# Output-weight sums on GpSimd, with later releases of their places and an earlier left sum

## The chip, the cores and the metric

The kernel runs on one core of one Trainium2 chip, in float32. The metric is the device time of one execution in microseconds (us). PE is TensorE, DVE is VectorE, ACT is ScalarE, POOL is GpSimd, SP is the engine whose queue issues the loads and stores spoken of here.

## The reference

Eight sequences of 448 rows go through an attention with 12 heads of 64, whose queries and keys are normalised, and then through a feed-forward network with a gate.

```python
def _attn_ref(q, k, v, g_q, g_k):                 # (8, 12, 448, 64)
    q_n, k_n = rmsnorm(q, g_q), rmsnorm(k, g_k)
    attn = softmax(q_n @ k_n.T / sqrt(64))
    return attn @ v

# bridge: (B,H,S,D) -> (B*S, H*D), 3584 x 768

def _moe_ref(x, w_gate, w_val, w_out, rms_g):     # 768 -> 1536 -> 768
    xn = x / rms(x) * rms_g
    g = xn @ w_gate
    return (silu(g) * (xn @ w_val)) @ w_out
```

## The kernel before

The function `safe_scores` writes the whole program in an order made by hand: each engine gets its instructions in the order in which the Python code emits them. `pe(fn)` emits one step of TensorE work and advances a counter `now["t"]`; `after(n, fn)` keeps a function back until n steps later. While the attention of one sequence is emitted, `fill` puts steps of the feed-forward network of the sequence before it between the attention's steps, so that TensorE always has work. The times below name these stages by what TensorE is doing for the network.

**Gate and value.** Sequence 0 uses the plain product. From sequence 1 on, four groups of columns are each computed by 15 block products in place of 18 (`PRODUCTS`, `three`, `product`, L1182). Nine of the 15 right operands are sums of weight blocks. They are made once, during sequence 1, by `derive` on DVE (L1087, L1090), stored to the DRAM scratch `kept` (L1095) and loaded from there by the later sequences. The left operands are sums of blocks of x, kept ready in the list `slow`.

**Output projection.** The stage of sequences 1 and 4 uses seven products in place of eight (`out_strassen`, L1447). Their right operands are the blocks B11, B21, B22 of the output weights and four sums T1 to T4. These sums, 4 for each of 6 columns, are made by `derive_o` (L1122) during sequence 1's gate stage and stored to `kept_o` by `keep` (L952). Their left operands are sums made from the list `first_sums` (16 of them in sequence 1, L1364, emitted from the end of the gate stage on), one after each step. Sequences 2, 3, 5, 6 and 7 apply the seven products once more inside each product (`out_quads`, L1518). Their right operands, the four-tile sums, are made by `derive_q` (L1150 to L1153) in 21 units of four subtractions, each followed by four stores to `kept_q` (L1157, L1160). The left operands S1 to S4 of that inner level are made by `left_q1` (L1392). For the tile i its steps come in the order a(i), d(i−1), b(i), c(i); d needs S4.

**Places and the load queue.** Weight blocks live in an arena of places. `ask` runs down a fixed list of loads (`uses`) and issues the next one on SP when `room(keep_free + 1)` says that enough places are free; it does so from `used`, one step or three after a place was given back by `give_back`. The list holds each sequence's gate loads (`wg`), then its output loads (`wo`, or `wq` for the two-level form). Loads of T sums wait until the sum's store has been emitted. The sources of the output sums (`wd`) and of the four-tile sums (`wx`) are loaded from another list, `side` (L1046); the loads of `uses` are L1066. Loads and stores share SP's queue, in order, and a store that waits for its data holds whatever stands behind it.

**The order inside `fill`.** After each step, `fill` makes at most one of the left sums, then `derive` if the attention's block began more than two steps ago, and, more than four steps after the block began, two `derive_o` if no `derive` was made, and one `derive_q`. `derive_q` returns at once while any output sum is still to be made.

Of the kernel before, what the change touches and what calls it, by code (L numbers as in the profile page):

```python
# [12 lines left out]
ALU = mybir.AluOpType  # L13
# [322 lines left out]
def safe_scores(  # L336
# [20 lines left out]
    nc = tc.nc  # L357
# [16 lines left out]
    st = {}  # L374


    now, due = {"t": 0}, []

    def after(n, fn):
        due.append((now["t"] + n, fn))  # L380
# [396 lines left out]
    slow, first_sums = [], []  # L777
# [109 lines left out]
    def data(key):  # L887
        return st[key][0][:, 0:GW if key[0] == "wg" else BW]
# [137 lines left out]
    asked = {"n": 0, "derived": 0}  # L1026
# [4 lines left out]
    derived = [(g, to) for g in GROUPS for _, _, to in PRODUCTS if to in RIGHT_G]  # L1031
# [6 lines left out]
    def ask():  # L1038

        if turn_of["n"] < TURNS:  # L1040
            return
        while side and (room(1, "side") or side[0][0] == "wd" and asked["derived"] > 32 and room(4, "wg")):
            key = side.pop(0)
            asked[key] = now["t"]
            st[key] = block("side" if room(1, "side") else "wg")
            nc.sync.dma_start(out=data(key), in_=home(key))  # L1046
        while asked["n"] < len(uses):
            key = uses[asked["n"]]
            kind, keep_free = "wg" if key[0] == "wg" else "w", 3
            if key[1] == 1 and key[0] == "wg":  # L1050
                kind, keep_free = "wg1", 6
            elif asked["derived"] < len(derived):
                return
            elif asked["n"] in next_gate:
                keep_free = 1
            if key[0] == "wo" and key[2][0] == "T" and ("kept", *key[2:]) not in asked:
                return
            if key[0] == "wq" and asked.get("sums_q", 0) < KG * (key[2] + 1):
                return
            if not room(keep_free + 1, kind):  # L1060
                return
            asked["n"] += 1
            asked[key] = now["t"]
            st[key] = block(kind)
            src = home(key)
            nc.sync.dma_start(out=data(key)[:, 0:src.shape[-1]], in_=src)  # L1066
# [43 lines left out]
    def derive_o(wait=4):  # L1110

        if not sums_o:
            return
        c, (to, plus, minus, place) = sums_o[0]
        for name in BLOCKS:
            if asked.get(("wd", 1, name, c), now["t"]) > now["t"] - wait:
                return
        sums_o.pop(0)
        a, b = data(("wd", 1, plus, c)), data(("wd", 1, minus, c))
        key = ("wd", 1, to, c)  # L1120
        st[key] = st[("wd", 1, place, c)]
        nc.vector.tensor_tensor(data(key), a, b, ALU.subtract)  # L1122

        def store():
            keep(key)
            asked["kept", to, c] = True

        after(2, store)
        if to == "T4":
            for name in ("T1", "T2", "T3", "T4"):  # L1130
                after(3, lambda name=name: used(("wd", 1, name, c)))

    todo_q = list(jobs_q)

    def derive_q(wait=5):

        if not todo_q or sums_o or now["t"] - asked.get("at_q", 0) < 3 or asked["n"] in next_gate or not room(2, "wg"):
            return False
        i, j = todo_q[0]
        keys = [("wx", 2, ORDER_Q[i], c) for c in (j, j + KG)]  # L1140
        for key in keys:
            if asked.get(key, now["t"]) > now["t"] - wait:
                return False
        todo_q.pop(0)
        own_a, own_b = ("ta", i, j), ("tb", i, j)
        st[own_a], st[own_b] = block("wg"), block("wg")
        asked["at_q"] = now["t"]
        x, y, ta, tb = (data(key).rearrange("p (h n) -> p h n", h=2) for key in (*keys, own_a, own_b))

        nc.vector.tensor_tensor(tb[:, 1], x[:, 1], x[:, 0], ALU.subtract)  # L1150
        nc.vector.tensor_tensor(ta[:, 1], y[:, 1], x[:, 1], ALU.subtract)
        nc.vector.tensor_tensor(ta[:, 0], y[:, 1], tb[:, 1], ALU.subtract)
        nc.vector.tensor_tensor(tb[:, 0], y[:, 0], ta[:, 0], ALU.subtract)  # L1153

        def store():
            parts = kept_q[i].rearrange("p (n w) -> p n w", w=HW)
            nc.sync.dma_start(out=parts[:, j], in_=x[:, 0])  # L1157
            for src, first, second in ((y, 1, 6), (ta, 2, 3), (tb, 4, 5)):
                gap = (second - first) * KG
                nc.sync.dma_start(out=parts[:, first * KG + j:second * KG + j + 1:gap], in_=src)  # L1160
            asked["sums_q"] = asked.get("sums_q", 0) + 1

        after(1, store)
        for key in (*keys, own_a, own_b):
            after(3, lambda key=key: used(key))
        return True

    def used(key):
        give_back(key)
        after(3 if key[0:2] == ("wg", 1) else 1, ask)  # L1170
# [213 lines left out]
    def left_q1(b, i, which):  # L1384

        of = lambda name: left_q(b, i, name)
        for at in which:
            to, first, second, what = (("S1", "A21", "A22", ALU.add), ("S2", "S1", "A11", ALU.subtract),
                                       ("S3", "A11", "A21", ALU.subtract), ("S4", "A12", "S2", ALU.subtract))[at]
            if to != "S3":  # L1390
                st["l2", b, i, to] = l2_pool.tile([128, S], F32, name="l2")[:, 0:KG * 128].rearrange("p (c n) -> p c n", c=KG)
            nc.vector.tensor_tensor(of(to), of(first), of(second), what)  # L1392
# [69 lines left out]
    def out_quads(b):  # L1462
# [77 lines left out]
        def bb(i):  # L1540
            ps = two(i, "b")
            u = st["u", b, i] = tmp.tile([128, S], F32, name="th", tag="th", bufs=2)[:, 0:BW].rearrange("p (h n) -> p h n", h=2)
            nc.vector.tensor_tensor(u[:, 0], ps[:, 0], st.pop(("q1", b, i)), ALU.add)
            nc.vector.tensor_tensor(u[:, 1], ps[:, 1], u[:, 0], ALU.add)
            if i == 0 or i > 1 and i + 1 < len(ORDER_Q):
                left_q1(b, i + 1, (0,))

        def c(i):
            ps = two(i, "c")
            u3 = st["u", b, i][:, 1:2].to_broadcast([128, 2, HW])  # L1550
            nc.vector.tensor_tensor(dst[i][1].rearrange("p (h n) -> p h n", h=2), ps, u3, ALU.add)
            left_q1(b, i, (3,))
            if i == 1:
                hurry(first_sums)
                left_q1(b, i + 1, (0,))
            if i + 1 < len(ORDER_Q):
                left_q1(b, i + 1, (1, 2))
            if i + 2 == len(ORDER_Q):
                st["l2 done", b] = True
# [70 lines left out]
    def fill(n=None):  # L1630

        if n is None:
            part["slot"] += 1
            upto = part["all"] * min(part["slot"] / part["slots"], 1.0)
            n = 0
            while n < len(todo) and part["spent"] + todo[n][0] / 2 < upto:
                part["spent"] += todo[n][0]
                n += 1
        for _ in range(min(n, len(todo))):
            _, turns, sums_made, fn = todo.pop(0)  # L1640
            while turn_of["n"] < turns:
                if not convert():
                    pe(idle)
            made, key = sums_made or (0, None)
            while asked["derived"] < made or (key and key not in st):
                before = dict(asked)
                derive(0)
                if key and key[0] == "wo":
                    derive_o(0)
                ask()  # L1650
                if before == asked:
                    pe(idle)
            pe(fn)
            convert()

            if first_sums:
                first_sums.pop(0)()
            elif slow and now["t"] - st["block"] > 4 and now["t"] - st["x_at"] >= NPAIR and may_make(slow[0][0]):
                slow.pop(0)[1]()
            if 2 < now["t"] - st["block"] < 5:  # L1660
                derive()
            if now["t"] - st["block"] > 4 and now["t"] != st.get("left_sums"):
                made = 0
                while made < 2:
                    done = derive()
                    if not done:
                        break
                    made += done
                for _ in range(0 if made else 2):
                    derive_o()  # L1670
                derive_q()

    def idle():
        pass
# [97 lines left out]
    for g in range(NG + 1):  # L1772
        b, hp = divmod(g, NPAIR)
# [138 lines left out]
```

## Time and profile before

| what | us |
|---|---|
| median of the runs | 1540.13 |
| the runs | 1535.95, 1540.13, 2208.22 |
| profiled execution | 1539.13 |
| its span | 1537.3 |
| TensorE busy in the span | 1487.0 |
| DVE busy | 1031.3 |
| GpSimd busy | 735.7 |
| the 24 output sums on DVE (L1122), from 300.5 to 426.0 | 15.3 |
| stage of sequence 1's gate and value | about 300 to 430 |
| stage of sequence 2's gate and value | about 530 to 627 |

The page of the profile gives for each engine its busy time. In the groups, `L1182 PE MATMUL ff<-raw,w` is line 1182's matmul that writes `ff` and reads `raw` and `w`; `x8` is a count. In the timeline each row has start and busy time, and in brackets the idle time of the engine just before it and what released it. In the waits, three numbers follow: total, times, longest. In the windows view each engine has busy time and number of instructions, in the order PE, weight loads, DVE, ACT, POOL, and then the granted TensorE clock (1.00 is full), the DMA engines' share and GB/s.

### The profile page before, as it was taken

Reading aid. Unit: us, or ns where it says so; the run is one execution under the profiler, and the core shown is the slowest. Engines: PE = TensorE matmul, PEld = TensorE weight load, DVE = VectorE, ACT = ScalarE, POOL = GpSimd, SP = SyncE. Lnnn points to the kernel's source line nnn. Section 1 sums busy time; section 2 is a strip of 40 time slices with the busy share of each in tenths; the row PEclk is TensorE's granted clock in tenths of the full one; section 3 lists DMA queues with packets and bytes.
Section 4 is the critical chain, followed back from the end, with each engine's and each line's share of the span. In section 5 each row is a group of like instructions: output and inputs, shape, how many; then the busy total and the mean of one; then the engine's idle time right before and its main releaser. Section 6 shows DMA issues by size and latency. Waiting matters only on the chain.

```text
span 1537.3 us, 25724 instructions
## 1 busy us (share of the span) xinstructions
PE 1487.0 (97%) x8732; PEld 1155.3 (75%) x8732; DVE 1031.3 (67%) x1826; ACT 603.2 (39%) x1377; POOL 735.7 (48%) x708
## 2 busy tenths in 40 slices
PE   8999999998899999899999999999999999999997
PEld 4344445686755887788888789858788789899997
DVE  5787999688854677784568644645668645684664
ACT  6856764343323443234442343334542343201110
POOL 6877987555423453364534545346544642021002
PEclk9999999999999999999999999999999999999999
DMA  7758585775578899986557765576457755597575
GB/s 204 227 151 247 164 250 172 233 248 186 188 226 237 280 287 286 304 268 191 160 149 235 242 195 161 163 223 198 128 164 236 228 161 144 157 290 232 172 229 177
DMA packets 302175, 322.50 MB, mean 210 GB/s; under 512 B 81620, under 2 KB 243668, under 8 KB 302036
## 3 DMA queue, kind: packets, MB, share of 16 engines
q1 hardware_dynamic: 301108, 320.58, 68.6%
q8 instruction: 72, 1.18, 0.3%
q14 instruction: 67, 0.55, 0.1%
q10 hardware_dynamic: 800, 0.20, 0.1%
q0 software_dynamic: 128, 0.00, 0.0%
HBM read 266.90 MB, written 53.77 MB: 209 GB/s over the span
## 4 chain that ended last, share of the span: by engine, by line
PE 82%; DVE 11%; issue 2%; DMA 2%; ACT 1%; POOL 1%; SPq 1%; DVEq 0%; POOLq 0%; ACTq 0%
PE ff L1182 37%; PE ff L1518 11%; PE sc L659 8%; PE av L674 7%; PE ff L1589 6%; PE ff L1447 5%; PE tr L545 2%; DVE l L1392 2%; PE ff L1320 1%; PE den L692 1%; PE sc L563 1%; PE den L607 1%; PE av L590 1%; DVE ms L496 1%; DVE w L1122 1%
## 5 line engine op out<-in xcount | busy, mean ns | idle before, releaser
L714 POOL TENSOR_TENSOR es<-es,e 128x448 f32<-128x448 f32 x205 | 251.6, 1227 | 13.6
L1182 PE MATMUL ff<-x,w 128*128 128x224 f32 x1272 | 254.2, 353 | 1.4 <-DVE pb L1203 1.1
L1182 PEld LDWEIGHTS ff<-x,w 128*128 128x128 f32 x1272 | 238.5, 190 | 4.5 <-issue 1.6
L659 PE MATMUL sc<-qT,kT 64*64 64x448 f32 x1176 | 231.6, 539 | 1.5 <-ACT rd L699 1.5
L674 PE MATMUL av<-e,vt 64*64 64x448 f32 x984 | 193.1, 538 | 0.0
L664 ACT ACTIVATE e<-sc 128x448 f32<-128x448 f32 x294 | 154.9, 546 | 75.9 <-PE sc L659 59.0
L1182 PE MATMUL ff<-xs,w 128*128 128x224 f32 x848 | 168.7, 353 | 4.9 <-DVE h L1215 1.6
L1182 PEld LDWEIGHTS ff<-xs,w 128*128 128x128 f32 x848 | 158.5, 190 | 8.9 <-issue 4.1
L644 POOL TENSOR_TENSOR ss<-ss,rd 128x448 f32<-128x448 f32 x40 | 46.8, 1170 | 216.8 <-ACT rd L643 213.4
L709 POOL TENSOR_TENSOR es<-e 128x448 f32<-128x448 f32 x41 | 47.1, 1148 | 201.6 <-ACT e L664 201.6
L659 PEld LDWEIGHTS sc<-qT,kT 64*64 64x64 f32 x1176 | 78.9, 132 | 83.5 <-issue 59.8
L1518 PE MATMUL ff<-w,l 128*128 128x192 f32 x630 | 118.9, 330 | 7.7 <-DVE l L1392 7.3
L1203 DVE TENSOR_TENSOR pc<-ff,l 128x448 f32<-128x448 f32 x56 | 34.9, 623 | 122.6 <-PE ff L1182 81.1
L515 POOL TENSOR_TENSOR rs<-ms,mhalf 128x12 f32<-128x12 f32 (+1 forms) x50 | 114.8, 2296 | 4.2
L1518 PEld LDWEIGHTS ff<-w,l 128*128 128x128 f32 x630 | 103.4, 190 | 15.9 <-DVE l L1392 13.8
L1589 PE MATMUL ff<-x,w 128*128 128x448 f32 x288 | 111.8, 541 | 0.0
L674 PEld LDWEIGHTS av<-e,vt 64*64 64x64 f32 x984 | 66.1, 133 | 41.4 <-issue 41.4
L1200 DVE TENSOR_TENSOR pb<-ff,pb 128x448 f32<-128x448 f32 x84 | 52.4, 623 | 65.2 <-PE ff L1182 55.9
L1589 PEld LDWEIGHTS ff<-x,w 128*128 128x128 f32 x288 | 53.3, 190 | 51.1 <-issue 47.6
L1182 PE MATMUL ff<-top_x,w 128*128 128x224 f32 x424 | 87.8, 357 | 2.8 <-DVE w L1090 2.8
L1182 PEld LDWEIGHTS ff<-top_x,w 128*128 128x128 f32 x424 | 78.8, 190 | 13.9 <-issue 11.6
L1182 PE MATMUL ff<-l,w 128*128 128x224 f32 x432 | 86.8, 353 | 1.1 <-DVE pc L1203 1.1
(210 smaller groups left out, 2809.3 us busy)
## 6 DMA issues: line engine op xcount, KB each, us to landing
w<-kept SPq DMA_DIRECT2D x383, 256.0 KB, 3.5
w<-kept_q SPq DMA_DIRECT2D x350, 192.0 KB, 3.8
w<-kept_o SPq DMA_DIRECT2D x150, 192.0 KB, 3.8
kept_q<-w SPq DMA_DIRECT2D x63, 192.0 KB, 3.9
qk<-in_q_dram SPq DMA_DIRECT2D x48, 192.0 KB, 3.8
qk<-in_k_dram SPq DMA_DIRECT2D x96, 96.0 KB, 4.0
raw<-in_moe_w_gate_dram SPq DMA_DIRECT2D x24, 384.0 KB, 4.7
raw<-in_moe_w_val_dram SPq DMA_DIRECT2D x24, 384.0 KB, 4.0
```

The costliest lines, as they stand in the source:

```text
L515: nc.gpsimd.tensor_tensor(st["rs", g][:, cols], ms, mhalf[:, cols], ALU.pow)
L644: after(m, lambda: (nc.gpsimd.tensor_tensor(ss, ss, rd, ALU.add), st.update({("summed", b): hp})))
L659: nc.tensor.matmul(ps[r, 0:S], lhsT=st["kT", g][r, keys_of(i)], rhs=st["qT", g][r, :], start=True, stop=True)
L664: nc.scalar.activation(e, ps[:, 0:S], ACT.Exp)
L674: nc.tensor.matmul(st["av", g][own(j), 0:S], lhsT=vt, rhs=st["e", g, i][r], start=i == 0, stop=i == PARTS - 1, skip_group_check=True)
L709: nc.gpsimd.tensor_tensor(st["es", g], st["e", g, 0], st["e", g, 1], ALU.add)
L714: nc.gpsimd.tensor_tensor(st["es", g], st["es", g], st["e", g, i], ALU.add)
L1182: nc.tensor.matmul(bank[:, w * HT:(w + 1) * HT], lhsT=data(key)[:, (2 * w + c) * 128:(2 * w + c + 1) * 128], rhs=a[left][:, c, :], start=o ...
L1200: nc.vector.tensor_tensor(T[name], ps[:, 0:S], T[name], ALU.add)
L1447: nc.tensor.matmul(ps, lhsT=left_o(b, which, LEFT_O[name], c), rhs=data(("wo", b, name, c)), start=first and c == 0, stop=c == NFP - 1, sk ...
L1518: nc.tensor.matmul(ps, lhsT=a[:, j, :], rhs=data(key)[:, n % 2 * HW:(n % 2 + 1) * HW], start=start and j == 0, stop=j == KG - 1, skip_grou ...
L1589: nc.tensor.matmul(bank[w][:, 0:S], lhsT=data(key)[:, c * 128:(c + 1) * 128], rhs=st["x", 0][:, 3 * half + c, :], start=half == c == 0, st ...
```

## The change

1. The subtraction of `derive_o` goes to GpSimd. It is made once after every step from the third of a block on, whether or not a `derive` was made in that step. The store follows four steps later (before: two), and the places of a column's sums are given back five steps after T4 (before: three).
2. The places of a unit of `derive_q` are given back after four steps (before: three).
3. `ask` may begin the output loads when at most two gate sums are still to be made (before: none), and these loads, and later those of sequence 1 other than B11's, keep six places free (before: three).
4. `left_q1(b, i, (3,))`, which makes S4, moves from the end of step c to the end of step b.
5. `fill` makes two of `first_sums` after a step while more than four of them are left.

```diff
--- before.py
+++ after.py
@@ -1049,10 +1049,14 @@
             kind, keep_free = "wg" if key[0] == "wg" else "w", 3
             if key[1] == 1 and key[0] == "wg":
                 kind, keep_free = "wg1", 6
+            elif asked["derived"] < len(derived) - 2:
+                return
             elif asked["derived"] < len(derived):
-                return
+                keep_free = 6
             elif asked["n"] in next_gate:
                 keep_free = 1
+            elif key[0:2] == ("wo", 1) and key[2] != "B11":
+                keep_free = 6
             if key[0] == "wo" and key[2][0] == "T" and ("kept", *key[2:]) not in asked:
                 return
             if key[0] == "wq" and asked.get("sums_q", 0) < KG * (key[2] + 1):
@@ -1119,16 +1123,16 @@
         a, b = data(("wd", 1, plus, c)), data(("wd", 1, minus, c))
         key = ("wd", 1, to, c)
         st[key] = st[("wd", 1, place, c)]
-        nc.vector.tensor_tensor(data(key), a, b, ALU.subtract)
+        nc.gpsimd.tensor_tensor(data(key), a, b, ALU.subtract)
 
         def store():
             keep(key)
             asked["kept", to, c] = True
 
-        after(2, store)
+        after(4, store)
         if to == "T4":
             for name in ("T1", "T2", "T3", "T4"):
-                after(3, lambda name=name: used(("wd", 1, name, c)))
+                after(5, lambda name=name: used(("wd", 1, name, c)))
 
     todo_q = list(jobs_q)
 
@@ -1162,7 +1166,7 @@
 
         after(1, store)
         for key in (*keys, own_a, own_b):
-            after(3, lambda key=key: used(key))
+            after(4, lambda key=key: used(key))
         return True
 
     def used(key):
@@ -1542,6 +1546,7 @@
             u = st["u", b, i] = tmp.tile([128, S], F32, name="th", tag="th", bufs=2)[:, 0:BW].rearrange("p (h n) -> p h n", h=2)
             nc.vector.tensor_tensor(u[:, 0], ps[:, 0], st.pop(("q1", b, i)), ALU.add)
             nc.vector.tensor_tensor(u[:, 1], ps[:, 1], u[:, 0], ALU.add)
+            left_q1(b, i, (3,))
             if i == 0 or i > 1 and i + 1 < len(ORDER_Q):
                 left_q1(b, i + 1, (0,))
 
@@ -1549,7 +1554,6 @@
             ps = two(i, "c")
             u3 = st["u", b, i][:, 1:2].to_broadcast([128, 2, HW])
             nc.vector.tensor_tensor(dst[i][1].rearrange("p (h n) -> p h n", h=2), ps, u3, ALU.add)
-            left_q1(b, i, (3,))
             if i == 1:
                 hurry(first_sums)
                 left_q1(b, i + 1, (0,))
@@ -1654,7 +1658,8 @@
             convert()
 
             if first_sums:
-                first_sums.pop(0)()
+                for _ in range(2 if len(first_sums) > 4 else 1):
+                    first_sums.pop(0)()
             elif slow and now["t"] - st["block"] > 4 and now["t"] - st["x_at"] >= NPAIR and may_make(slow[0][0]):
                 slow.pop(0)[1]()
             if 2 < now["t"] - st["block"] < 5:
@@ -1666,9 +1671,9 @@
                     if not done:
                         break
                     made += done
-                for _ in range(0 if made else 2):
-                    derive_o()
                 derive_q()
+            if now["t"] - st["block"] > 2:
+                derive_o()
 
     def idle():
         pass
```

## The prediction

> **What bounds the kernel now.** I began with the page's busy times.
>
> ```profile
> PE 1487.0 (97%) x8732; PEld 1155.3 (75%) x8732; DVE 1031.3 (67%) x1826; ACT 603.2 (39%) x1377; POOL 735.7 (48%) x708
> ```
>
> PE (TensorE) has only 50.3 us of 1537.3 to lose, some 9 of them the tail, and the change takes no matmul away. So I followed the timeline of PE from end to end and listed its idle gaps: they sum to 41.5 us. Three places bear on the change. The first is the gate/value stage of sequence 1 (300 to 430 us), where the output sums are made. The waits of PE in that stretch:
>
> ```profile
> PE ff L1182 <- DVE pb L1200: 2.8, 2, 2.4
> PE ff L1182 <- DVE w L1090: 2.8, 1, 2.8
> PE ff L1447 <- DMA w<-kept_o: 1.9, 1, 1.9
> ```
>
> (total us, times, longest.) PE idles 15.2 us there, mostly behind DVE. What DVE did ahead of the 2.8, from the timeline (start, busy):
>
> ```profile
> 345.94 1.50 DVE L1090 TENSOR_TENSOR raw<-raw,w 128x512 f32<-128x512 f32 x1
> ...
> 357.54 2.64 DVE L1122 TENSOR_TENSOR w<-w 128x384 f32<-128x384 f32 x4
> ...
> 361.80 0.68 DVE L1090 TENSOR_TENSOR w<-w 128x512 f32<-128x512 f32 x1
> ```
>
> Four output sums (L1122) stood ahead of the gate sum that PE needed at 362.6. The windows view says how full DVE is (third number: busy in 25 us; fifth: POOL):
>
> ```profile
> 300.00:325.00 25.00, 22.28 (x144) 17.88 (x144) 23.82 (x39) 10.77 (x25) 11.45 (x12) 1.00 0.70 234
> ...
> 400.00:425.00 25.00, 22.34 (x131) 19.02 (x124) 22.94 (x36) 7.73 (x19) 15.44 (x13) 1.00 0.41 138
> ```
>
> The second place is the end of sequence 2's gate stage, where the four-tile sums (L1150 to L1153) are still being made:
>
> ```profile
> 619.07 0.36 DVE L1150 TENSOR_TENSOR w<-w 128x192 f32<-128x192 f32 x1 [2.25 <-DMA kept_q<-w]
> ...
> 621.57 3.35 PE L1182 MATMUL ff<-raw,w 128*128 128x224 f32 x8 [4.38 <-DVE pb L1200]
> ```
>
> DVE waited 2.25 us for a store to leave the place it writes; PE then stood 4.38 us, and its next 8 matmuls took 3.35 us where eight at full clock take 1.68. SP's waits from 500 to 640 show the same stores holding the load queue:
>
> ```profile
> SPq L1046 <- DMA kept_q<-w: 12.5, 11, 3.1
> ```
>
> The third is the stalls for left sums in the two-level output stages, from PE's waits over the whole span:
>
> ```profile
> PE ff L1518 <- DVE l L1392: 7.3, 17, 1.2
> ```
>
> By PE's gaps it is about 1.6 us in each of four of the five stages, 8.2 in all with those that the view puts down to `raw`; where I looked closer (0.53 at 654.99) the waiting step is d, whose left operand is S4.
>
> **Two rules of the Trainium skill.** SBUF — State Buffer, section "SBUF: two separate sides", says that DVE with two SBUF inputs and GpSimd take a shared port pair as an exclusive lock for a whole instruction, and the second blocks. The trace agrees in direction: a 128x512 DVE sum takes 0.69 us alone and 1.50 beside a GpSimd operation (+0.81), while DVE additions with a PSUM operand stay at 0.62. I go by the trace's +0.81. TensorE: Matmul & The Clock Gate, Part 1, "What's actually happening", says that the clock halves after an idle window of about 3.4 us. Here a gap of 2.77 us alone left the clock at 1.00; the 4.38 halved it (0.51 in the window 620 to 625), and 2.44 followed by 1.86 did too (0.76 in 430 to 435). I go by the trace: a pair of gaps near 4 us in sum may cost 1.7 to 2.7 us on top.
>
> **Part by part, against the profiled execution, 1539.13 us** (span 1537.3 and 1.8 around it).
>
> *24 sums to GpSimd.* From DVE: 24 x 0.639 = 15.3 us. To GpSimd: the nearest row is L1489, an addition of the same 128x384, 0.99 to 1.38 us; I take 1.1; 24 x 1.1 = 26 us. GpSimd is busy 61.5 of the 125 us from 300 to 425, so it has room. But each of the 24 may lengthen a DVE sum by up to 0.81; if half of that happens, DVE loses 10 of its 15.3 us again. The net relief is 5 us of DVE time. PE's gaps straight behind L1122 are 1.08 + 2.77 + 2.44 = 6.3; with a third of the relief kept I take 2 off. Bounds: −5 (all gone but the port's toll), +3 (full toll of 19.4 against 15.3, none of it hidden).
>
> The stores behind these sums wait longer, two steps more, and SP is in order, so queued behind a store that waits for GpSimd are the gate loads of sequence 1 (8 us ahead of their use or more: hidden) and at the end the load of B11, column 5, which PE already awaits at 427.93. The last two sums would end at about 425.6 by my count of GpSimd's queue from 403; store, then load at 426, landing at 428.5: +0.6 (0 to +3). The clock drop there stays.
>
> *Later output loads of sequence 1.* Columns wait until 6 places are kept free, not 3. Laying the changed instruction order on PE's times of before, four loads are asked for late: T3 column 4 at 458.7, the moment of its use (before: 11.7 us earlier), T1 column 1 also at its use, T4 column 4 only 2.9 us and B22 column 4 5.0 us ahead. And SP is then busy with stores of the four-tile sums. The mechanism is in the trace of before (SP's queue and DVE):
>
> ```profile
> 457.85 0.36 DVE L1153 TENSOR_TENSOR w<-w 128x192 f32<-128x192 f32 x1
> ...
> 458.82 0.94 SPq L1046 DMA_DIRECT2D w<-kept_o  x2
> 459.81 0.42 SPq L1157 DMA_DIRECT2D kept_q<-w  x1
> 460.28 2.64 SPq L1160 DMA_DIRECT2D kept_q<-w  x3
> 463.02 2.36 SPq L1066 DMA_DIRECT2D w<-kept_o  x5
> ```
>
> A load that is issued at about 460 lands 3.6 us later (median of w<-kept_o), at 463.5: PE stands 463.5 − 458.7 = 4.8 us. T1 column 1 likewise, with the store done sooner: 3.2. T4 column 4: 1.2. B22: 0.7. Sum 9.9 us, and one clock drop, 2.5. Total +12.4. Bounds: +2 (SP drains before, and only landings shorter than the median remain), +14 plus 2.7.
>
> *Four-tile sums sooner, and their places a step longer.* The block derivations finish sooner, so these 21 units start about 22 us earlier (at 434.8, not 457.1) and end near 593.6, not 627.2. What stood at 619 to 621 is gone: −4.38, and −2.7 of half clock, −7.1. SP's 12.5 us behind kept_q<-w shrink, since a place kept one step longer has its store done when it is reused; that feeds the wg loads whose stalls at 589 and 592 are 1.63 + 1.12. Against it, the step longer leaves fewer free places, and three wg loads come to 5.4 to 7 us ahead of use, against a landing of 3.5 to 5: just covered; if SP lags by the 4 to 9.5 us seen at 560 to 612, not. Net −8 (−10 to 0).
>
> *S4 one step sooner.* Its sum then follows the b step's two additions, not c's, so PE's step c and the next a (12 products and 2.1 us each at 652 to 654) cover it: −6 (−8.2 to −2: c's own addition, which other steps need, may move back by one sum of 0.55).
>
> *Two first sums per step:* 0. These are the left sums of sequence 1's output stage (L1364, 0.55 us each); DVE idles 1.2 to 2.4 us between its additions there, and two of them cost 1.1. Without that cover a product's addition would come 0.55 later.
>
> Sum: −2 + 0.6 + 12.4 − 8 − 6 = −3.0. 1539.13 − 3.0 = **1536.1 us**. The median shown is 1540.13, 1.0 above the profiled run, and the lowest 1535.95.
>
> **Rivals.**
> *A: the late loads land in time.* For: SP's queue was free before 456.9, and a PE that is delayed a little makes SP relatively earlier. Against: the request itself stands one step from its use, and landing alone is 3.6. The 12.4 falls to about 2: 1539.13 − 2 + 0.6 + 2 − 8 − 6 = 1525.7.
> *B: the load queue ends late (slower).* One mechanism: SP's in-order queue between 435 and 490, where stores of four-tile sums now stand beside loads asked for at their use. If SP lags there as it does at 560 to 612, 4 to 9.5 us, each of the four loads pays about 4.5 more: 4 x 4.5 = 18; 1536.1 + 18 = 1554. It ends slower than before once the lag is over about 0.8 us per load (3.0/4). For: the 6.45 us that SP spent at L1160 at 452. Against: these are waits for DVE, which is emptier there (13.8 of 25 us).
> *C: the port gives back what GpSimd takes.* The full toll, +3 in place of −2, with B11's load 3 us later instead of 0.6: 1536.1 + 5 + 2.4 = 1543.5. For: 24 GpSimd operations where DVE is 95% busy. Against: some 26 us of DVE's work there has a PSUM operand (L1200, L1203), and GpSimd stands idle half of the time.
>
> **Chances.** Forecast 0.40, A 0.27, B 0.18, C 0.15. The range runs from A's far end (A with S4's full 8.2 and the relief's 5 is 1520.5) to B with a little more lag: 1519 to 1557. A run can tell 2%, 31 us, from no change; no case reaches that alone: faster 0.03, slower 0.06 (B with a lag near 8 us per load), same 0.91.
>
> **What would show it.** Right: no PE gap over 1 us at L1518 behind L1392; no 4.38 us gap and no half clock at the end of sequence 2's gate stage; L1126 on POOL at about 1.1 us each; new `PE ff L1447 <- DMA w<-kept_o` of 5 to 12 us at 440 to 490. Wrong: no such new DMA stall (then A), one of over 15 us (then B), or DVE's L1087 and L1090 lengthened to 1.2 us and more on the mean with PE's gaps at 300 to 430 grown (then C).

## The result, and the profile after

The changed kernel takes 1556.11 us (median; 1554.71 to 1560.42), the kernel before 1538.28 in the comparison: a ratio of 1.0122, 95% interval 1.0104 to 1.014. It is some 18 us slower, where 1536.1 was forecast. One run of before at 2208.22 is a disturbed execution and enters no ratio. The profiled execution of the changed kernel took 1556.04 us with a span of 1554.2, 16.9 more than before.

Lines after L1048 have moved down by 4 to 5: the output sums are L1126, the four-tile sums L1154 to L1157 with stores L1161 and L1164, `product` is L1186, the outputs L1451 and L1522, S1 to S4 L1396, first sums L1368, loads of `uses` L1070.

The busy times of the page:

```profile
PE 1492.7 (96%) x8732; PEld 1159.2 (75%) x8732; DVE 1034.3 (67%) x1802; ACT 602.7 (39%) x1377; POOL 767.6 (49%) x732
```

DVE lost 24 instructions and yet is busy 3.0 us longer: in the same 1554 us other operations of it took more time. PE is busy 5.7 us longer with the same 8732 matmuls, since it spends more time at half clock (a granted clock of 0.50). The rest, 11.2 us, is idle time. In the waits of PE over the span (total, times, longest) the first has grown, from one wait of 1.9 us before, and the others were not there before:

```profile
PE ff L1451 <- DMA w<-kept_o: 11.6, 4, 5.3
PE sc L659 <- DVE x L744: 8.0, 3, 2.7
...
PE ff L1522 <- DVE pa L1556: 2.3, 4, 0.8
```

PE's order is the same in both kernels, so the k-th matmul of one can be set against the k-th of the other. How far the changed kernel is behind at each (times in the left column are those of before):

| up to | what | us behind | step |
|---|---|---|---|
| 30 | start-up | 1.4 | +1.4 |
| 420.67 | gate stage of sequence 1 | 4.1 | +2.7 |
| 432.95 | B11's load, with half clock | 7.4 | +3.3 |
| 489.05 | loads of T and B22 sums, with half clock | 19.0 | +11.6 |
| 521.86 | the stage's rest | 19.5 | +0.5 |
| 626.45 | end of sequence 2's gate stage | 8.7 | −10.8 |
| 638.71 | scores behind L744 | 11.3 | +2.6 |
| last matmul | two-level stages | 15.3 | +4.0 |
| end of the span | the last stores | 16.9 | +1.6 |

The 1.4 us at the start are not the change's: the profiled executions of this study lie between 0.2 us ahead of before's and 3.0 behind it there, though their programs are alike in that part. The windows view shows which parts are clock (the number before the last two is the granted TensorE clock):

```profile
435.00:440.00 5.00, 5.00 (x9) 2.58 (x9) 4.89 (x12) 0.48 (x1) 0.00 (x0) 0.50 0.91 242
835.00:840.00 5.00, 4.66 (x21) 3.87 (x22) 1.11 (x3) 0.97 (x2) 0.68 (x1) 0.66 0.62 184
```

Each follows one of the new gaps: PE works without pause from 435 to 440 and gets through 9 matmuls. The window after the gap that ends at 471.52 shows 0.59, and the one after 1183.78 shows 0.66.

**The late load.** The chain that ended last, cut to 464 to 474, reads like a diagram of the stall (start, length, what):

```profile
463.85 0.61 DVE xs L772
464.46 0.27 DVE w L1154
...
465.30 0.35 DVE w L1157
...
465.75 0.41 SPq L1164
...
466.22 0.48 SPq L1046
...
467.29 4.18 DMA w<-kept_o
...
471.52 2.94 PE ff L1451 x4
```

SP had a store of four-tile sums at the head of its queue, whose data DVE finished at 465.65; DVE came to it only then, since an addition ahead of it (L1416, 463.38) had waited 2.38 us for PE. Then two loads of other tiles went first, and the load that PE needed (SP's line L1070) was issued at 467.29 and landed 4.18 us later. The wait goes round: PE, DVE, SP, DMA, PE.

**The held bank.** The timeline ahead of the first gap at L659:

```profile
645.14 1.37 DVE L1368 TENSOR_TENSOR h<-top,h 128x384 f32<-128x384 f32 x1
646.44 1.49 DVE L1368 TENSOR_TENSOR raw<-top,raw 128x384 f32<-128x384 f32 x1
647.85 0.34 DVE L1542 TENSOR_TENSOR y<-ff,th 128x192 f32<-128x192 f32 x1
648.12 0.66 DVE L744 SCALAR_TENSOR_TENSOR x<-x,rg,rb 128x448 f32<-128x448 f32 x1
648.70 0.62 DVE L1368 TENSOR_TENSOR raw<-h,h 128x384 f32<-128x384 f32 x1
649.25 0.67 DVE L744 SCALAR_TENSOR_TENSOR x<-x,rg,rb 128x448 f32<-128x448 f32 x1
...
649.97 0.59 PE L659 MATMUL sc<-qT,kT 64*64 64x448 f32 x2 [2.66 <-DVE x L744]
```

`norm_x` puts `rb` in a bank (one of the buffers that matmuls write) of the PSUM pool of four that the scores `sc` use too. Six scalings L744 read that bank, one emitted per step, and it comes free with the sixth. Before, three sums L1364 stood among the scalings, and the sixth ended at 638.65, just as PE came at 638.71:

```profile
637.98 0.67 DVE L744 SCALAR_TENSOR_TENSOR x<-x,rg,rb 128x448 f32<-128x448 f32 x1
```

With two first sums per step, five of them (L1368) stand there, two lengthened to 1.37 and 1.49 us beside GpSimd's operations (L714, 1.38 us each), and PE waits.

### The profile page after: what moved, and what is told of

It reads as the page before. It is cut to its first block, busy times and chain, and to the rows that moved or that the text cites. A ratio compares the mean times of both kernels' runs of the same rounds, so it can differ in the third digit from the quotient of the medians.

```text
span 1554.2 us, 25712 instructions
## 1 busy us (share of the span) xinstructions
PE 1492.7 (96%) x8732; PEld 1159.2 (75%) x8732; DVE 1034.3 (67%) x1802; ACT 602.7 (39%) x1377; POOL 767.6 (49%) x732
## 4 chain that ended last, share of the span: by engine, by line
PE 78%; DVE 11%; DMA 4%; POOL 3%; issue 2%; SPq 1%; ACT 1%; DVEq 0%; POOLq 0%; ACTq 0%
PE ff L1186 35%; PE ff L1522 11%; PE av L674 7%; PE sc L659 6%; PE ff L1593 6%; PE ff L1451 4%; PE tr L545 2%; DVE l L1396 1%; DMA w<-kept_o 1%; PE den L692 1%; PE ff L1324 1%; PE den L607 1%; PE sc L563 1%; DVE x L744 1%; POOL es L714 1%
## 5 line engine op out<-in xcount | busy, mean ns | idle before, releaser
L714 POOL TENSOR_TENSOR es<-es,e 128x448 f32<-128x448 f32 x205 | 252.1, 1230 | 13.1
L1186 PE MATMUL ff<-x,w 128*128 128x224 f32 x1272 | 254.3, 353 | 0.6 <-DVE pc L1207 0.3
L659 PE MATMUL sc<-qT,kT 64*64 64x448 f32 x1176 | 232.5, 540 | 9.5 <-DVE x L744 8.0
L1186 PEld LDWEIGHTS ff<-x,w 128*128 128x128 f32 x1272 | 238.4, 190 | 3.8 <-issue 1.4
L1186 PE MATMUL ff<-xs,w 128*128 128x224 f32 x848 | 168.4, 353 | 3.1 <-issue 1.6
L1186 PEld LDWEIGHTS ff<-xs,w 128*128 128x128 f32 x848 | 158.7, 190 | 6.7 <-issue 4.4
L659 PEld LDWEIGHTS sc<-qT,kT 64*64 64x64 f32 x1176 | 79.0, 133 | 91.9 <-issue 59.8
L1522 PE MATMUL ff<-w,l 128*128 128x192 f32 x630 | 120.9, 335 | 4.7 <-DVE pa L1556 2.3
L515 POOL TENSOR_TENSOR rs<-ms,mhalf 128x12 f32<-128x12 f32 (+1 forms) x50 | 114.9, 2298 | 4.2
L1522 PEld LDWEIGHTS ff<-w,l 128*128 128x128 f32 x630 | 106.2, 194 | 11.5 <-DVE pa L1556 3.5
L1493 POOL TENSOR_TENSOR y<-y,pa 128x384 f32<-128x384 f32 x10 | 11.3, 1154 | 159.6 <-DVE y L1568 150.5
L1186 PE MATMUL ff<-top_x,w 128*128 128x224 f32 x424 | 88.1, 357 | 1.5 <-ACT l L1201 0.7
L1186 PEld LDWEIGHTS ff<-top_x,w 128*128 128x128 f32 x424 | 78.6, 190 | 13.2 <-issue 8.5
```

Of the source, the lines that this page charges most:

```text
L515: nc.gpsimd.tensor_tensor(st["rs", g][:, cols], ms, mhalf[:, cols], ALU.pow)
L659: nc.tensor.matmul(ps[r, 0:S], lhsT=st["kT", g][r, keys_of(i)], rhs=st["qT", g][r, :], start=True, stop=True)
L714: nc.gpsimd.tensor_tensor(st["es", g], st["es", g], st["e", g, i], ALU.add)
L1186: nc.tensor.matmul(bank[:, w * HT:(w + 1) * HT], lhsT=data(key)[:, (2 * w + c) * 128:(2 * w + c + 1) * 128], rhs=a[left][:, c, :], start=o ...
L1522: nc.tensor.matmul(ps, lhsT=a[:, j, :], rhs=data(key)[:, n % 2 * HW:(n % 2 + 1) * HW], start=start and j == 0, stop=j == KG - 1, skip_grou ...
```

## The experiments

Every ratio is to the kernel before, with its 95% interval. A signed number after it is the difference of the medians, in us, from the kernel that was edited: the changed kernel (1556.11), or the kernel before in the same series (1537.9 to 1538.5). "Edit n" is number n of the change as listed. What is said of a stage is read from the one profiled execution of each run, against that of before and with the start-up taken off.

**One first sum per step again (a_fs1).**

```diff
-                for _ in range(2 if len(first_sums) > 4 else 1):
-                    first_sums.pop(0)()
+                first_sums.pop(0)()
```

> The changed kernel with one first sum per step again (edit 5 undone). Theory Q (the additions put ahead of the x scaling in DVE's queue hold the PSUM bank that the scores wait for): the three gaps of 2.66 us before L659 behind L744 at 650, 835 and 1184 go, and the half clock after two of them (1.4 and 1.6 us), so about 11 us: 1556 to 1545, ratio to the kernel before about 1.005. Theory P (GpSimd's sums and the shared port are the cost everywhere, and those gaps would be replaced by others in the same place): within 2 us of 1556.

1549.79 us, 1.0071 (1.0051 to 1.0092): −6.3. All three gaps at L659 and their half clock are gone, 9.6 us on PE's times from 626 to the last matmul. Against that, the stretch of the late loads cost 2.2 us more in the profiled execution (half clock from 482.1 to 488.9, where the changed kernel had none) and the gate stage 1.1 (half clock from 304.6 to 308.0). Edit 5 is confirmed as the source of the three gaps, and the theory that the port alone makes them falls. That it is the bank which holds PE is tested by the scalings below.

**Three places kept free (a_kf3).**

```diff
-            elif key[0:2] == ("wo", 1) and key[2] != "B11":
-                keep_free = 6
```

> The changed kernel with three places kept free for sequence 1's output loads in place of six (only that clause of edit 3 undone). Theory Q: the late requests at 471 and 482 come earlier, the gaps of 5.27, 1.76 and 0.75 us go and the half clock after 471 too: 12 us less, about 1544. Rival R (the stores of four-tile sums hold SP whatever the number of places, since each waits for DVE, which waits for PE): the loads are asked for sooner but stand behind the same stores; less than 4 us off.

1544.96 us, 1.0045 (1.0028 to 1.0062): −11.2. No load of `kept_o` makes PE wait after 435. Since the stores still stand in SP's queue, rival R falls: what mattered was that the request came at its use. Part was given back: PE waits 1.91 us at 621 behind DVE, and 0.2 to 1.2 us at 647 to 662 behind loads from `kept_q`. The six places had a use that the prediction did not name: with them the four-tile sums end at 612, with three at 656.

Of edit 3 this clause alone was undone. That the output loads may begin two gate sums sooner was not run alone, and what it does is not shown.

**Edit 5 alone (b_fs2)**, in the kernel before, the reverse of the first diff.

> The kernel before with two first sums per step while more than four are left (edit 5 alone). Theory Q: three new gaps of about 2.7 us before L659 behind L744 and half clock after some of them: +8 to +11 us, about 1548. Theory P: no change, 1538.

1545.72 us, 1.0041 (1.0029 to 1.0053): +7.4. Two gaps of 2.67 us at 825 and 1174, half clock after each, none at 638: fewer than the three expected, the size a little under. At 638 the same five sums stand among the scalings, but at 0.55 to 0.65 us each: the fourth began at 637.74, 0.02 us ahead of GpSimd's operation, and it was that one which lengthened (1.54 us, where the same took 1.14 at 820). At 820.7 and 822.0 GpSimd was first, and two of the sums take 1.36 and 1.49 us. So the order of the sums makes the wait possible, and how many of them come second to GpSimd sets its size.

**S4 sooner, alone (b_s4).**

```diff
             nc.vector.tensor_tensor(u[:, 1], ps[:, 1], u[:, 0], ALU.add)
+            left_q1(b, i, (3,))
...
-            left_q1(b, i, (3,))
```

> The kernel before with S4 made at the end of step b (edit 4 alone). Theory Q: step d no longer waits for S4 but for c's addition, which reads the bank that d adds to; the gaps fall from 8.2 to about 4: -4 us, about 1534. Rival: the wait changes its name and not its length: 1538.

1534.74 us, 0.9976 (0.9968 to 0.9984): −3.6. PE's waits at L1518 over the span, where before 17 waits for L1392 alone summed to 7.3:

```profile
PE ff L1518 <- DVE pb L1552: 3.0, 3, 1.0
PE ff L1518 <- DVE pa L1552: 1.7, 4, 0.5
PE ff L1518 <- DVE l L1392: 1.3, 2, 1.1
```

Part of the wait only changed its name: step d adds into the bank that c's addition (L1552) reads, so it can't start before that addition, which S4 now stands ahead of. In the profiled execution the two-level stages gain 2.8 us. It also has no half clock at 429, where before had 3.4 us of it; that is 1.7 us which the edit does not explain.

**Both clauses undone (a_fs1_kf3)**, the first two diffs together.

> The changed kernel with both clauses undone: one first sum per step, and three places free. If the two costs are separate they add: 1556.1 - 6.3 - 11.2 = 1538.6. If the places kept free had a use later (the w<-kept_q gaps at 647 to 665 and the 1.91 us at 621 that came with three places), they don't add: about 1542.

1541.81 us, 1.0025 (1.0015 to 1.0035): −14.3 where the two alone sum to −17.5. Nearly separate: the 3.2 us that are missing lie where the six places had their use. In its profile a gap of 3.86 us at L659 behind L744 appears at 639 with one first sum per step: a unit of four-tile sums, begun at 634.88, stands ahead of the sixth scaling there, another cause for the same held bank. With six places these units are over by then.

**Edit 2 alone (b_q4).**

```diff
-            after(3, lambda key=key: used(key))
+            after(4, lambda key=key: used(key))
```

> The kernel before with the places of the four-tile sums kept one step longer (edit 2 alone). Theory S (DVE waited for the store to leave the place it writes): DVE L1150's wait of 2.25 us at 619 and PE's 4.38 behind it go, and the half clock after it: -5 to -7 us, about 1532. Theory E (what helped was the earlier start of these units, which the output sums' new order gives): the gap at 621 stays within 1.5 us of 4.4; 1538, or up to 3 us more since fewer places are free for the gate loads.

1539.26 us, 1.0006 (0.9995 to 1.0018): no change. Yet PE is 9.0 us ahead at 617 in its profile. DVE's wait for the store ahead of L1150 fell from 2.25 us to 0.44, and PE's gap of 4.38 has become 2.21. Of the 9.0, 5.2 are lost again 16 us later and after (timeline):

```profile
628.57 1.29 DVE L1150 TENSOR_TENSOR w<-w 128x192 f32<-128x192 f32 x1
...
632.30 0.36 DVE L1153 TENSOR_TENSOR w<-w 128x192 f32<-128x192 f32 x1
632.58 0.67 DVE L744 SCALAR_TENSOR_TENSOR x<-x,rg,rb 128x448 f32<-128x448 f32 x1
...
633.31 0.59 PE L659 MATMUL sc<-qT,kT 64*64 64x448 f32 x2 [3.86 <-DVE x L744]
```

The last unit of four-tile sums, three of them 1.28 us apiece beside GpSimd where the fourth took 0.36, stands ahead of the sixth scaling, and PE waits for the bank. In the changed kernel these units are over by then. The 3.8 us that this execution keeps to its last matmul are not seen in the median. Theory S holds for half of the gap, and not for the sum.

**The output sums on DVE in the changed kernel (a_dve).**

```diff
-        nc.gpsimd.tensor_tensor(data(key), a, b, ALU.subtract)
+        nc.vector.tensor_tensor(data(key), a, b, ALU.subtract)
```

> The changed kernel with the output sums on DVE again, one per step as changed (only the engine of edit 1 undone). Theory G (the sums on GpSimd cost more than they give: port toll in the gate stage, and SP waiting for them at the end): the gaps at 304 (2.38), 329 (2.50) and 434 (3.77, with 1.4 us of half clock) fall to the sizes of before: -3 to -6 us, about 1551. Theory D (GpSimd relieves DVE as the prediction had it): +2 to +6 us, about 1560.

1554.33 us, 1.0097 (1.0073 to 1.0121): its interval overlaps that of the changed kernel. Inconclusive on the total. In its profiled execution the gate stage costs 2.4 us, where the changed kernel's costs 2.7, so GpSimd gave no relief there; from 420.67 to 438 it gains 0.8, where the changed kernel loses 3.3 at B11's load.

**The output sums on GpSimd in the kernel before (b_gp)**, the reverse of that diff.

> The kernel before with the output sums on GpSimd, in pairs as before and with nothing else changed (only the engine of edit 1). Theory G: +2 to +6 us from the port toll and from stores that now wait for GpSimd two steps after, about 1542. Theory D: -2 us or more, about 1535, since 15.3 us leave DVE.

1547.29 us, 1.0063 (1.0044 to 1.0083): +8.8, more than either theory. The gate stage got no longer (2.0 us behind at 420, 3.0 at the start). The loss that its profiled execution shows, 6.4 us from 420.67 to 438, is one wait of PE for B11's load and the half clock after it:

```profile
PE ff L1447 <- DMA w<-kept_o: 8.2, 1, 8.2
```

The rest of the 8.8 is not placed. GpSimd ran eight of the sums in one row, and SP stood at their stores ahead of the load (timelines of GpSimd and SP):

```profile
425.65 10.26 POOL L1122 TENSOR_TENSOR w<-w 128x384 f32<-128x384 f32 x8
```

```profile
427.05 6.67 SPq L952 DMA_DIRECT2D kept_o<-w  x6
433.77 0.92 SPq L1066 DMA_DIRECT2D w<-kept_o  x2
```

**x scalings two per step in the changed kernel (a_x2).**

```diff
-                after(hp // 3 if b == 1 else hp, lambda hp=hp: scale(hp))
+                after(hp // 3 if b == 1 else hp // 2, lambda hp=hp: scale(hp))
```

> The changed kernel with the six x scalings (L744) of sequences 2 to 7 emitted two per step instead of one, so that fewer of DVE's other sums stand between them; edit 5 stays. If the PSUM bank that L744 reads last is what the scores wait for, the three gaps of 2.66 us at 650, 835 and 1184 go with their half clock: -8 to -11 us, about 1546, the same as undoing edit 5. If DVE as a whole is late there, the gaps move to another line and less than 3 us is won.

1545.41 us, 1.0044 (1.003 to 1.0059): −10.7, with edit 5 still in. No wait for L744 is left. The lengthened sums are still there, behind the last pair of scalings instead of ahead of it:

```profile
644.70 1.27 DVE L744 SCALAR_TENSOR_TENSOR x<-x,rg,rb 128x448 f32<-128x448 f32 x2
...
651.28 1.49 DVE L1368 TENSOR_TENSOR raw<-top,raw 128x384 f32<-128x384 f32 x1
```

That holds the bank as the cause and not DVE's load; one new gap, 2.58 us at L1522 at 1356 (before this edit 0.81), is its price.

**Edit 2 with the same scalings (b_q4_x2).**

> The kernel before with edit 2 alone and the x scalings two per step. With edit 2 alone PE was 9 us ahead at 626 and lost 3.86 us and some half clock at 633 behind L744. If that bank is the cause, the 633 gap goes and 7 to 9 us stay: about 1530, ratio 0.995. If DVE is simply behind by its four-tile sums, PE waits as long for another DVE operation: 1538.

1535.69 us, 0.9985 (0.9976 to 0.9994): −2.7, 3.6 less than edit 2 alone. The 3.86 at 633 is gone. Less stays than the 7 to 9 expected: 0.99 us at a load from `kept_q` at 645 and 1.99 at L1518 at 1338 are new. The scalings in pairs were not run alone in the kernel before, so what they do by themselves there is not shown.

**Edits 2 and 4 with the scalings (b_s4_q4_x2).**

> The kernel before with edits 2 and 4 and the x scalings two per step; without GpSimd's sums, the six places and the two first sums. If the parts add: 1538.4 - 8 - 4 = 1526, ratio 0.992. If the S4 gain and the four-tile gain share a stage, 1530.

1531.67 us, 0.9967 (0.9955 to 0.9979): faster than both kernels, by 6.8 and 24 us. The parts add: −2.7 with edit 2 and the scalings, −3.6 with edit 4. Less than the 12 expected, since 8 was put down for the first of them; the same 1.99 us at L1518 is there, at 1334.

**Three places and the scalings in the changed kernel (a_kf3_x2).**

> The changed kernel with three places free for sequence 1's output loads and the x scalings two per step. Three places alone gave 1545; two gaps of 2.66 us at 826 and 1174 and half clock after them are left there: -7 us, about 1538. If the gaps at 621 to 665 (DVE and w<-kept_q) grow in turn, 1542.

1540.37 us, 1.0013 (1.0003 to 1.0023): −15.7, between the two figures. Both gaps at L659 that three places alone had left are gone; those at 645 to 665, most behind loads from `kept_q`, grew, the longest to 2.07 us.

**Edit 1's order alone, on DVE (b_one), and on GpSimd (b_one_gp).**

```diff
-        after(2, store)
+        after(4, store)
...
-                for _ in range(0 if made else 2):
-                    derive_o()
                 derive_q()
+            if now["t"] - st["block"] > 2:
+                derive_o()
```

with the release of the T places after five steps in place of three; `b_one_gp` has GpSimd's subtraction besides.

> The kernel before with the output sums in the changed order, one after each step, store and release two steps later, but on DVE and with nothing else changed. If the order costs (a sum stands beside each gate sum): the gate stage of sequence 1 gets 2 to 3 us longer, and the four-tile sums end sooner, so the 4.38 us gap at 621 falls to below 2: together 1533 to 1537. If the order is free and GpSimd is what costs: the gate stage as before and 1531.

> The whole of edit 1 in the kernel before: the same order on GpSimd. If GpSimd pays through the stores that SP waits for (B11's load at 428 to 436): about 3 to 5 us over the same order on DVE, of it 1.5 to 6 at that load and less than 1 in the gate stage. If GpSimd relieves DVE: 2 us under it.

1541.27 us, 1.0024 (1.0013 to 1.0034), and 1542.25, 1.0027 (1.0015 to 1.0039). Alike in total, and not alike inside. By PE's times, with the start-up taken off, the order costs 4.0 us in the gate stage up to 420.67 on DVE and 2.3 on GpSimd. The difference of 1.7 is one stretch of half clock, 3.4 us from 328.2, that only the execution with DVE has. Then B11's load takes back more than that: from 420.67 to 438 the one on DVE gains 1.0, and the one on GpSimd loses 3.3, with a gap of 3.80 against 0.86 and half clock after it.

The other profiled executions say the same. The gate stage is 2.3 to 4.2 us longer in all nine runs that have the order, whichever engine makes the sums; with the engine alone (b_gp) it is 1.0 shorter. B11's load costs 3.1 to 3.3 in six of the seven runs with the order on GpSimd, and neither of the two on DVE loses anything there. So the order costs, and the store behind GpSimd's sums costs. Relief of DVE in the gate stage is 1.7, −0.3 and 1.0 us in the three pairs that differ by the engine alone, which is no more than one stretch of half clock, and so it is not shown.

The earlier end of the four-tile sums, expected from this order, did not come: the gap at 621 is 4.15 and 4.03 in these two. The units begin 19 us sooner than before and end 33 us later:

```profile
L1150 DVE TENSOR_TENSOR w<-w x21: 345/351/360, 437.7 to 658.4; 128x192 f32<-128x192 f32 x21
```

## Why the prediction was wrong, point by point

**The sums (−2.0 forecast, +2.7 measured).** The step priced the engine and not the order. It let 24 sums leave DVE and kept the gate stage otherwise as it was, but the change also makes one sum after every step, beside the gate sums instead of in the steps without one. That costs 4.0 us on DVE, 1.7 of them half clock (b_one), and 3.3 on GpSimd (b_one_gp against b_gp). A relief of 2 us by the engine is neither shown nor excluded. The duration guessed, 1.1 us, was 1.23:

```profile
L1126 POOL TENSOR_TENSOR w<-w 128x384 f32<-128x384 f32 x24 | 29.5, 1229 | 4.2 <-DMA w<-kept_o 3.6
```

Rival C's full toll is not seen: the mean of the gate sums rose from 0.81 to 0.83 us (28 of L1091) and from 0.84 to 0.97 (32 of L1094), some 4.6 us in all where 19.4 would be full. (The bound of +3 for the full toll should have been +4.1, which is 19.4 − 15.3.)

**B11's load (+0.6 forecast, +3.3).** The mechanism was named and its size missed. The last two sums were counted to end at 425.6; GpSimd ran the last four from 428.61 to 433.73, behind L515 and L520, whose 2.3 and 1.35 us came first. And "the clock drop there stays" was wrong: before, half clock lasted from 429.0 to 432.4; after the longer gap of 3.77 it cost 1.4 us more.

**The late loads (+12.4 forecast, +11.6).** Right in mechanism, and in size as a sum: 5.27 + 1.76 + 0.75 = 7.8 us of gaps where 9.9 were worked out, and 3.8 of half clock where 2.5 were; undoing the clause took 11.2 us off. The load at 471.52 is the one expected at 458.7, and it waited 5.27 where 4.8 was worked out. The prediction had SP's store waiting for DVE; it did not have DVE waiting for PE's product first. Three gaps came where four were expected.

**The four-tile sums (−8 forecast, −10.8).** The gap of 4.38 and its half clock went, and the 3.8 us at 573, 589 and 592 shrank to 0.7. The size came out and half of the reason did not. Keeping the place longer does most of it (−8.9 between 489 and 626 in b_q4's profile). The other half, units that end early because the block derivations finish sooner, failed: the order lets them begin at 438 and end at 659 (b_one). In the changed kernel they end at 612, where 593.6 was forecast and 626 was before, and that is the work of the six places of edit 3: three pairs of runs that differ in that clause alone end at 612 to 615 with it and at 656 to 660 without. The step saw those places only as the cost of the late loads:

```profile
L1154 DVE TENSOR_TENSOR w<-w x21: 346/350/855, 438.0 to 611.2; 128x192 f32<-128x192 f32 x21
```

What the step also left out is what would be late next: with edit 2 alone, the same units stand ahead of L744, and over half of the gain is lost there.

**S4 (−6 forecast, −3.6).** The wait is not gone but changed in part to c's addition; the step asked what S4 waits for and not what else d waits for.

**Two first sums per step (0 forecast, about +7).** The largest error, and the step that failed. It was costed at nothing with one place looked at, sequence 1's output stage at 452 to 464, where DVE has idle time; that place does cost nothing (0.0 us from 438 to 489 in b_fs2). But `left_sums` fills the same list in the two-level stages too, where five such sums stand among the x scalings in place of three, and there it cost 7.4 us alone (b_fs2) and 6.3 when undone (a_fs1). The trace of before held the warning: the last L744 ended at 638.65 and PE began the score at 638.71, a cover of nothing. Together with S4 this part was forecast at −6, and PE's times give +6.6 from 626.45 to the last matmul: 12.6 of the 19.9 us by which the forecast, −3.0, missed the 16.9 of the profiled executions.

**Rival B** named the slow side, 1554, by more lag at the four loads. The time came out near it, and just inside the range that was given, by luck: the loads cost what the forecast gave them, and the held bank, the gate stage's order and B11's load made up the rest.

**The clock (1.7 to 2.7 us for a pair of gaps near 4).** A gap of 2.66 us was followed by half clock at 835 and 1184 and not at 650. TensorE: Matmul & The Clock Gate, Part 1, "What's actually happening", of the Trainium skill describes a free-running window of 3413 ns, and the traces here show it: the granted clock changes only at whole multiples of 3.41 us from its first change in each execution. For each of the three gaps in the changed kernel, the window in which PE worked least, and for the second also the window after it:

```profile
648.38:651.79 3.41, 1.82 (x13) 1.11 (x14) 1.54 (x3) 0.74 (x2) 1.86 (x2) 1.00 0.65 200
...
832.70:836.11 3.41, 0.77 (x8) 0.21 (x8) 2.59 (x5) 0.54 (x1) 2.83 (x3) 1.00 0.40 103
836.11:839.52 3.41, 3.41 (x14) 3.18 (x11) 0.82 (x2) 0.97 (x2) 0.00 (x0) 0.50 0.50 156
...
1180.86:1184.27 3.41, 0.75 (x12) 0.21 (x8) 2.87 (x5) 0.69 (x2) 3.11 (x3) 1.00 0.33 82
```

At 835 and 1184 the gap fell inside one window, and PE was busy for 0.77 and 0.75 us of it; at 650 it was shared by two, with 1.82 us of PE in the emptier one.

## What to carry to other kernels

Price an edit in every stage in which its line runs, and ask of each instruction put ahead on an engine what buffer the ones behind it release, above all a PSUM bank shared with the matmuls. A store that waits for a slow engine costs nothing until a load that is needed stands behind it in the same queue; count where the last such store ends. A gap that vanishes gives its time only if the next consumer is ready sooner too: edit 2 was 9 us ahead and lost 5.2 of them within 20. And a clause that costs in one stage can pay in another: the six places made loads late at 471 and ended the four-tile sums 44 us sooner.

## What the runs showed of the hardware that was not expected

GpSimd beside DVE slowed a short DVE sum far more than a long one in proportion: a 128x192 sum went from 0.36 to 1.28 us (+0.92, L1150 in b_q4), a 128x512 one from 0.69 to 1.50 (+0.81, L1090 in the kernel before). In b_q4 the three slow sums went one to each of three GpSimd operations, 1.25 us each:

```profile
628.31 3.75 POOL L714 TENSOR_TENSOR es<-es,e 128x448 f32<-128x448 f32 x3
```

So such a sum takes about as long as the GpSimd operation beside it, whatever its own length. That fits the lock for a whole instruction that SBUF — State Buffer of the Trainium skill states in "SBUF: two separate sides" better than slower parallel work.

What decides on the clock is the share of one 3.41 us window in which PE was busy, not the length of a gap. Of the 7091 windows at full clock in the 16 profiled executions, each one with PE busy below 0.42 of it was followed by half clock, none above 0.53 was, and between the two it went either way. After a window at half clock the next was at full clock where PE had been busy for 0.914 of it or more, and at half again for 0.912 or less. The skill's section speaks of an idle window; here a window with PE busy for 0.22 of it sufficed. One window at half clock under steady work costs 1.7 us.

It follows that the same gap can cost 1.7 us or nothing, by where it falls. The start of the kernel varied by 3.2 us between profiled executions, and the time of the first lasting full clock with it (5.75 us in before, 13.14 in b_gp). So a profile of one execution can be off by some 4 us from the median of its kernel (a_x2: 1549.46 against 1545.41), and a difference of one window between two profiles, as at 328 in b_one, is not a finding.
